# Attention and expert layers on one core: Q and K laid out transposed on the host, loaded where the scores read them, and the eighth applied to K in place

## The chip, the cores and the metric

The kernel runs on one core of a Trainium2 chip. The metric is device microseconds (us) of one execution. The time before the change is the median of three runs, 510.81 us (510.80 to 510.99). Engines are named as in the profile: PE is TensorE (PEld is its weight load), DVE is VectorE, ACT is ScalarE, POOL is GpSimd, SP is SyncE, which here only issues transfers.

## The reference

Three layers follow each other. Only the first is touched by the change.

```python
# attention: batch 2, 12 heads, 448 positions, 64 numbers per head
scores = (1 / sqrt(64)) * matmul(q, k.transpose(0, 1, 3, 2))   # the factor is 0.125, "the eighth"
scores = where(causal_mask, -1e9, scores)
attn = exp(scores - max(scores)) / (sum + 1e-9)
x = matmul(attn, v)                                            # then to 896 tokens x 768
# a top-1 layer of 8 experts: x -> gate * (relu(x @ w1[e]) @ w2[e])
# a dense layer: max(x @ w1, x @ w2, x @ w3) @ w_out
```

## The kernel before

The kernel has three stages on PE: attention (0 to about 131 us, with the first expert's first layer mixed into its end), the experts (to about 310 us) and the dense layer (to the end).

**Pairs.** Attention goes through 12 pairs of heads. K, Q and V come from the host as one tile per pair. `load(p)` (L455) makes the tiles `kr` and `qr` (112 partitions, 4 blocks of positions, 2 heads of 64) and issues their transfers from SP (L462); `loadv(p)` (L464) issues that of `vr`. A transfer into a tile that is used again waits on SP until its last reader is done, and everything behind it on SP waits too: transfers of the next pairs, of V, of the dense layer's first weights (token `D..x`) and of the experts' weights (`L0`, `L1`).

**Transposes.** The scores need both operands with the 64 head numbers on the partitions. `tk` (L473) transposes K in four blocks on PE into a PSUM bank, `tk_out` (L479) copies it to the tile `kt` (128 partitions: two heads of 64, 448 positions) by ACT or DVE (`put`, L483 to L487). `tq` (L489) does the same with Q, and `tq_out` (L495) copies it in two halves, times 0.125, into `qbd`: a block-diagonal tile of 7 blocks of 128 x 128, head 0 in the upper left quarter of each block, head 1 in the lower right one, so that one matmul serves both heads. There are three `qbd` tiles, used in turn; their other quarters are zeroed once (L434, L439), the whole tile being cleared.

**Scores and softmax.** `scores` (L510) multiplies the blocks of `qbd` with the front part of `kt`, in four groups (token `S0` to `S3`), and adds the mask. `row_max` on DVE (`M`), `row_exp` on ACT (`E`) and `row_rec` on DVE (`R`) follow, then `nrm` (`N0` to `N6`, L540), which divides a block of rows in place: on DVE, or on POOL where the token ends in p. `ptr` (`T0` to `T3`, L544) transposes the result on PE in four groups, `ptr_out` (`t`) copies it out, `av` (`A`) multiplies with V, `xtok` (`X`) transposes back, and `xtok_out` (L581) copies and sends the tokens to DRAM through POOL's queue (L587).

**Order.** Nothing is planned by the program: `SCHEDULE` (L18) is an order written by hand, one line for each step of the loop at L770, and every engine works its own instructions off in that order. A token is a digit (which pair, counted from the line's base `max(p - 2, -1)`), a letter (the function, chosen in `emit` at L724) and an argument (the group, then the PSUM tag or the engine). `1Qa 1K 1qss 1ks` is thus: transpose Q and K of pair 0, copy Q by ACT twice, copy K by ACT. `EA` and `EM` prepare the router's expert vectors on DVE and ACT. Before the loop, pairs 0 to 3 are loaded (L693 to L702); line p loads pair p + 3 and V of pair p + 2.

```python
    for p, line in enumerate(SCHEDULE[:-1]):
        if 0 < p < NP - 3:
            load(p + 3)
        if 2 <= p < NP - 2:
            loadv(p + 2)
        for tok in line.split():
            emit(max(p - 2, -1), tok)
```

Of the kernel before, what the change touches and what calls it, by code (L numbers as in the profile page):

```python
# [7 lines left out]
F32 = mybir.dt.float32  # L8
# [7 lines left out]


SCHEDULE = (  # L18
# [19 lines left out]
def kernel(  # L38
# [15 lines left out]
    nc = tc.nc  # L54
# [31 lines left out]
    def bank(tag, name, bufs=None):  # L86
        return ps.tile([P, 512], F32, tag=tag, name=name, bufs=bufs)
# [341 lines left out]
        poff.append(o)  # L429
        o += P * ((i + 2) // 2)  # L430
    PW = o
    qbd = [eb.tile([P, NQ, P], F32, name=f"qbd{i}") for i in range(3)]
    prb = [p.tile([P, PW], F32, name=f"prb{i}") for i, p in enumerate((eb, ab))]
    nc.vector.memset(qbd[0], 0.0)  # L434
    for t in prb:
        for i in range(0, NQ, 2):
            nc.vector.memset(t[:, poff[i] + 64 * (i + 1):poff[i] + 64 * (i + 2)], 0.0)
    for t in qbd[1:]:
        nc.gpsimd.memset(t, 0.0)  # L439

    pairs = [(b, hp) for b in range(B) for hp in range(HP)]
    NP = len(pairs)
# [11 lines left out]

    def load(p):  # L455
        b, hp = pairs[p]
        kr = eb.tile([TB, 4, 2, D], F32, tag="kr", name="kr", bufs=3)
        qr = eb.tile([TB, 4, 2, D], F32, tag="qr", name="qr", bufs=3)
        vr = ab.tile([P, 4, 2, D], F32, tag="vr", name="vr", bufs=4)
        raw[p] = (kr, qr, vr)  # L460
        for t, s in ((kr, k), (qr, q)):
            nc.sync.dma_start(out=t.rearrange("p c j d -> p (c j d)"), in_=s[p])  # L462

    def loadv(p):  # L464
        b, hp = pairs[p]
        vr = raw[p][2]
        nc.sync.dma_start(out=vr.rearrange("p c j d -> p (c j d)"), in_=v[p])

    held = {}

    BUFS = {"t": 3, "h": 1, "a": 2, "b": 2}

    def tk(p, tag):  # L473
        kr = raw[p][0]
        ps = held["k", p] = bank(tag, "psk", BUFS[tag])
        for c in range(4):
            nc.tensor.transpose(ps[:, c * TB:(c + 1) * TB], kr[:, c].rearrange("p j d -> p (j d)"), ident[:TB, :TB])

    def tk_out(p, eng):  # L479
        ktt[p] = eb.tile([P, S], F32, tag="kt", name="kt", bufs=3)  # L480
        put(eng, ktt[p], held.pop(("k", p))[:, :S])

    def put(eng, out, in_):  # L483
        if eng == "v":
# [1 line left out]
        else:  # L486
            nc.scalar.copy(out=out, in_=in_)  # L487

    def tq(p, tag):  # L489
        qr = raw[p][1]  # L490
        ps = held["q", p] = bank(tag, "psq", BUFS[tag])
        for c in range(4):
            nc.tensor.transpose(ps[:, c * TB:(c + 1) * TB], qr[:, c].rearrange("p j d -> p (j d)"), ident[:TB, :TB])

    def tq_out(p, eng):  # L495
        ps = held.pop(("q", p))
        t = qbd[p % 3]
        for h in range(2):
            r = slice(64 * h, 64 * h + 64)
            x = ps[r, :S].rearrange("p (i c) -> p i c", c=64)  # L500
            if eng[h] == "v":
                nc.vector.tensor_scalar(out=t[r, :, r], in0=x, scalar1=0.125, scalar2=None, op0=ALU.mult)
            else:
                nc.scalar.mul(out=t[r, :, r], in_=x, mul=0.125)

    SG = ((6,), (5, 0), (4, 1), (3, 2))
    SC = {6: 0, 5: 1, 0: 2, 4: 3, 1: 4, 3: 5, 2: 6}
# [2 lines left out]
    def scores(p, g, tag):  # L510
        if p not in sms:
            sms[p] = sm_p.tile([P, 3, 8], F32, tag="sm", name="sm")
        ps = held["s", p, g] = bank(tag, "pss", BUFS[tag])
        for i in SG[g]:
            n, o = 64 * (i + 1), SO[i]
            nc.tensor.matmul(ps[:, o:o + n], lhsT=qbd[p % 3][:, i], rhs=ktt[p][:, :n], start=i == SG[g][0], stop=False, skip_group_check=True)  # L516
        for i in SG[g]:
            o = SO[i] + 64 * i
            nc.tensor.matmul(ps[:, o:o + 64], lhsT=identb, rhs=maskb, start=False, stop=i == SG[g][-1], skip_group_check=True)  # L519
# [35 lines left out]
    done = {}  # L555

    def av(p, kt, tag):
        vr = raw[p][2]
        if kt == 0:
            held["a", p] = bank(tag, "psa", BUFS[tag])  # L560
            done[p] = 0
        ps = held["a", p]
        nb = NQ - 2 * kt
        base = sum(NQ - 2 * n for n in range(kt))
        kk = 64 if kt == 3 else P
        done[p] += 1
        for j in range(2):
            nc.tensor.matmul(ps[64 * j:64 * j + 64, P * kt:S], lhsT=vr[:kk, kt, j],
                             rhs=ptt[p][:kk, base:base + nb, 64 * j:64 * j + 64],
                             start=(kt == 0), stop=(done[p] == 4), skip_group_check=True)  # L570
# [153 lines left out]
    def emit(p, tok):  # L724
# [5 lines left out]
        elif tok[0] == "W":  # L730
            wsplit(int(tok[1]), int(tok[2]), int(tok[3]), tok[4])
        elif tok[0] == "D":
            u, c = int(tok[1]), 384 * int(tok[2])
            if tok[3:] == "":
                held[tok] = dw_dec(u, held.pop(tok + "a"), c, c + 384, 384)
            elif tok[3] == "a":
                held[tok] = magnitude(dwt[u][0], c, c + 384, 384)
            elif tok[3] == "l":
                held.pop(tok[:3])()
            else:  # L740
                dw_load(u)
        elif tok[0] == "H":
            held["S0"].L1(int(tok[1]), [int(tok[2])])
        else:
            p += int(tok[0])
            f, a = tok[1], tok[2:]
            if f == "S":
                scores(p, int(a[0]), a[1:] or "t")
            elif f == "M":
                row_max(p, int(a))  # L750
            elif f == "E":
                row_exp(p, int(a))
            elif f == "R":
                row_rec(p)
            elif f == "N":
                nrm(p, int(a[0]), nc.gpsimd if a[1:] else nc.vector)
            elif f == "T":
                ptr(p, int(a[0]), a[1:] or "a")
            elif f == "t":
                ptr_out(p, int(a[0]), a[1])  # L760
            elif f in "KQX":
                {"K": tk, "Q": tq, "X": xtok}[f](p, a or "b")
            elif f == "A":
                av(p, int(a[0]), a[1:] or "b")
            elif f == "q":
                tq_out(p, a)
            else:
                {"k": tk_out, "a": av_out, "x": xtok_out}[f](p, a)

    for p, line in enumerate(SCHEDULE[:-1]):  # L770
        if 0 < p < NP - 3:
# [327 lines left out]
def packed(name, a):  # L1099
# [1 line left out]
    import numpy as np  # L1101

    if name in ("q", "k"):
        a = a.reshape(2, 6, 2, 4, 112, 64).transpose(0, 1, 4, 3, 2, 5).reshape(12, 112, 512)
    elif name == "v":
        a = np.pad(a.reshape(2, 6, 2, 448, 64), ((0, 0), (0, 0), (0, 0), (0, 64), (0, 0)))
        a = a.reshape(2, 6, 2, 4, 128, 64).transpose(0, 1, 4, 3, 2, 5).reshape(12, 128, 512)
# [31 lines left out]
```

## Time and profile before

| | us |
|---|---|
| median of three runs | 510.81 |
| the profiled execution, own time | 510.31 |
| its span, first to last instruction | 508.6 |
| PE busy in the span | 487.9 (96%) |
| DVE busy | 334.2 (66%) |
| ACT busy | 280.0 (55%) |
| POOL busy | 47.5 (9%) |

The profiled execution is 0.50 us below the median, and 1.7 us of it lie outside the span. A row of a group of instructions gives their count, busy time and the mean duration of one; a row of the waits gives who waited for whom; a row of the timeline gives the start, the busy time and the number of instructions merged into it; a row of windows gives each engine's busy time in a stretch, with the number of instructions in brackets, the granted PE clock, the share of the DMA engines and GB/s.

### The profile page before, as it was taken

What the parts mean: (1) busy time and instruction counts of PE and PEld (TensorE: products, weight loads), DVE (VectorE), ACT (ScalarE), POOL (GpSimd) and SP (SyncE); (2) the same over time, 40 slices, a digit from 0 to 9 for tenths busy, and PEclk for the clock granted to TensorE, in tenths of its full rate; (3) what the DMA queues carried; (4) which work ended last, traced back from release to release, by engine and by line L of the source; (5) the groups of instructions that cost most, each with busy time, mean ns of one, the idle gap of its engine ahead of it and who ended that gap; (6) DMA issues with size and microseconds to landing.
All of it is one profiled execution on the core that took longest, in us unless ns stands there. A gap on an engine that the chain in (4) does not pass through costs nothing. (4 is left out here: it accounts for less than half of the span.)

```text
span 508.6 us, 8597 instructions
## 1 busy us (share of the span) xinstructions
PE 487.9 (96%) x2858; PEld 423.4 (83%) x2858; DVE 334.2 (66%) x692; ACT 280.0 (55%) x587; POOL 47.5 (9%) x71
## 2 busy tenths in 40 slices
PE   5999999999999999999999999699999999999994
PEld 4777676776789899889889888599999999999994
DVE  4899857997556398511398891489899898841000
ACT  5878878988643598623588882444453444411000
POOL 4321111211100000000011000000000000000111
PEclk9999999999999999999999999799999999999998
DMA  8552343931013798113898850744353440000111
GB/s 208 156 196 75 97 131 113 399 130 39 18 64 101 308 336 301 43 32 112 307 327 329 327 218 3 301 152 172 124 188 132 149 153 1 1 0 32 63 63 62
DMA packets 17788, 75.83 MB, mean 149 GB/s; under 512 B 2360, under 2 KB 2360, under 8 KB 17728
## 3 DMA queue, kind: packets, MB, share of 16 engines
q1 hardware_dynamic: 15328, 65.31, 36.3%
q0 software_dynamic: 2400, 9.83, 5.8%
q8 instruction: 24, 0.39, 0.3%
q14 instruction: 36, 0.29, 0.2%
HBM read 69.62 MB, written 5.51 MB: 148 GB/s over the span
## 5 line engine op out<-in xcount | busy, mean ns | idle before, releaser
L965 PE MATMUL pm<-x2h,dwh 128*128 128x448 f32 x204 | 75.0, 367 | 0.0
L967 PE MATMUL pm<-x2h,dwl 128*128 128x448 f32 x204 | 74.5, 365 | 0.0
L966 PE MATMUL pm<-x2l,dwh 128*128 128x448 f32 x204 | 74.4, 365 | 0.0
L971 PE MATMUL l<-w2h,hh 128*128 128x384 f32 x160 | 56.4, 352 | 0.7 <-ACT hh L207 0.7
L971 PE MATMUL l<-w2l,hh 128*128 128x384 f32 x160 | 53.8, 336 | 0.0
L242 DVE TENSOR_TENSOR w1l<-raw,w1h 128x768 fp32r<-128x768 f32 x40 | 36.4, 952 | 24.1 <-PE l L971 19.7
L516 PE MATMUL pss<-kt,qbd 128*128 128x320 f32 (+6 forms) x168 | 46.7, 397 | 1.3 <-ACT prb L530 1.3
L971 PE MATMUL l<-w1h,xhp 128*128 128x512 f32 x109 | 43.9, 403 | 0.0
L530 ACT ACTIVATE prb<-pss,sm 128x64 f32<-128x64 f32 (+6 forms) x84 | 39.5, 480 | 6.8 <-DVE sm L523 6.5
L971 PE MATMUL l<-w1l,xhp 128*128 128x512 f32 x109 | 43.2, 396 | 0.0
L967 PEld LDWEIGHTS pm<-x2h,dwl 128*128 128x128 f32 x204 | 38.2, 187 | 3.7
L174 ACT CAST dwh<-dt_t 128x768 fp32r<-128x768 f32 (+1 forms) x20 | 15.5, 773 | 46.6 <-DVE dt_t L173 46.6
L966 PEld LDWEIGHTS pm<-x2l,dwh 128*128 128x128 f32 x204 | 38.3, 188 | 3.3
L965 PEld LDWEIGHTS pm<-x2h,dwh 128*128 128x128 f32 x204 | 38.3, 188 | 3.2
L523 DVE TENSOR_REDUCE sm<-pss 128x1 f32<-128x448 f32 (+6 forms) x84 | 31.6, 414 | 9.7 <-PE pss L519 9.2
L971 PE MATMUL l<-w2h,hl 128*128 128x384 f32 x160 | 36.4, 337 | 0.3 <-DVE hl L210 0.3
L242 DVE TENSOR_TENSOR w2l<-raw,w2h 128x768 fp32r<-128x768 f32 x40 | 35.2, 952 | 0.9 <-ACT w2h L241 0.7
L516 PEld LDWEIGHTS pss<-kt,qbd 128*128 128x128 f32 x168 | 28.6, 194 | 8.5 <-ACT prb L530 1.8
L241 ACT CAST w1h<-raw 128x768 fp32r<-128x768 f32 x40 | 32.1, 844 | 0.0
L971 PE MATMUL l<-w1h,xlp 128*128 128x512 f32 x109 | 31.3, 394 | 0.0
L971 PEld LDWEIGHTS l<-w2h,hh 128*128 128x128 f32 x160 | 30.1, 188 | 1.4 <-ACT hh L207 1.0
L971 PEld LDWEIGHTS l<-w2l,hh 128*128 128x128 f32 x160 | 30.2, 189 | 0.4
(263 smaller groups left out, 1009.8 us busy)
## 6 DMA issues: line engine op xcount, KB each, us to landing
raw<-in_moe_w_dram SPq DMA_DIRECT2D x48, 768.0 KB, 7.2
rawd<-in_moe_w_dram SPq DMA_DIRECT2D x18, 768.0 KB, 5.4
rawd<-in_moe_w_out_dram SPq DMA_DIRECT2D x6, 768.0 KB, 5.3
vr<-in_v_dram SPq DMA_DIRECT2D x12, 256.0 KB, 4.9
kr<-in_k_dram SPq DMA_DIRECT2D x12, 224.0 KB, 4.4
qr<-in_q_dram SPq DMA_DIRECT2D x12, 224.0 KB, 3.4
xd<-xall POOLq DMA_DIRECT2D x12, 224.0 KB, 3.1
xrp<-xd,idx POOLq DMA_INDIRECT x11, 5.1
```

Source lines behind the costliest of these rows:

```text
L174: nc.scalar.copy(out=hi[:, c0:c1], in_=f)
L241: nc.scalar.copy(out=hi[:, sl], in_=r[:, sl])
L242: nc.vector.tensor_tensor(out=lo[:, sl], in0=r[:, sl], in1=hi[:, sl], op=ALU.subtract)
L516: nc.tensor.matmul(ps[:, o:o + n], lhsT=qbd[p % 3][:, i], rhs=ktt[p][:, :n], start=i == SG[g][0], stop=False, skip_group_check=True)
L523: nc.vector.tensor_reduce(out=sms[p][:, 0, SC[i]:SC[i] + 1], in_=held["s", p, g][:, SO[i]:SO[i] + 64 * (i + 1)], axis=AX.X, op=ALU.max, ne ...
L530: nc.scalar.activation(out=prb[p % 2][:, poff[i]:poff[i] + n], in_=ps[:, SO[i]:SO[i] + n], func=AF.Exp, bias=sm[:, 0, SC[i]:SC[i] + 1], sc ...
L965: nc.tensor.matmul(o, lhsT=lh, rhs=rh, start=first, stop=False)
L966: nc.tensor.matmul(o, lhsT=lh, rhs=rl, start=False, stop=False)
L967: nc.tensor.matmul(o, lhsT=ll, rhs=rh, start=False, stop=last)
L971: nc.tensor.matmul(o, lhsT=a, rhs=b, start=first and n == 0, stop=last and n == len(ops) - 1)
```

## The change

K and Q come from the host with the 64 head numbers on the rows (12 x 128 x 448). K's transfer writes `kt` itself, now in four buffers; two transfers write the two quarters of `qbd`, of which there are four, in pieces of 64 numbers. The transposes and their copies go. The factor 0.125 is applied to `kt` in place by a new function `scale` (token `q`): on DVE for pairs 0 and 1, on POOL for the ten others, where it stands first in its line (`4qp`, for the pair loaded one line earlier; `3qp` in line 0). Only the quarters of `qbd` that stay zero are cleared: two half-tile memsets for each of the four, on DVE for the first, on POOL for the others.

```diff
-    "1Qa 1K 1qss 1ks EA 2K 1S0 1M0 2Qa EM 2ks 1S1 1E0 2qss 1M1 1E1 1S2 1M2 1E2 3Kh 1S3 3kv 1M3 1E3 2S0a 3Qh",
-    "2M0 1R 1N2p 1N1 2S1 2M1 2E0 3qss 4K 2E1 2S2 1N0 1N6p 1N3 2M2 4ks 1N4 1N5 4Qh 1T0 2S3 1T1b 1t0v D00x 2M3 4qss 2E2 3S0 ET 1T3 1t1s",
+    "1qv 2qv 3qp EA 1S0 1M0 EM 1S1 1E0 1M1 1E1 1S2 1M2 1E2 1S3 1M3 1E3 2S0a",
+    "4qp 2M0 1R 1N2p 1N1 2S1 2M1 2E0 2E1 2S2 1N0 1N6p 1N3 2M2 1N4 1N5 1T0 2S3 1T1b 1t0v D00x 2M3 2E2 3S0 ET 1T3 1t1s",
...
-    qbd = [eb.tile([P, NQ, P], F32, name=f"qbd{i}") for i in range(3)]
+    qbd = [eb.tile([P, NQ, P], F32, name=f"qbd{i}") for i in range(4)]
...
-    nc.vector.memset(qbd[0], 0.0)
+    for n, t in enumerate(qbd):
+        for j in range(2):
+            (nc.gpsimd if n else nc.vector).memset(t[64 * j:64 * j + 64, :, 64 - 64 * j:128 - 64 * j], 0.0)
...
-    for t in qbd[1:]:
-        nc.gpsimd.memset(t, 0.0)
...
-        kr = eb.tile([TB, 4, 2, D], F32, tag="kr", name="kr", bufs=3)
-        qr = eb.tile([TB, 4, 2, D], F32, tag="qr", name="qr", bufs=3)
-        vr = ab.tile([P, 4, 2, D], F32, tag="vr", name="vr", bufs=4)
-        raw[p] = (kr, qr, vr)
-        for t, s in ((kr, k), (qr, q)):
-            nc.sync.dma_start(out=t.rearrange("p c j d -> p (c j d)"), in_=s[p])
+        ktt[p] = eb.tile([P, S], F32, tag="kt", name="kt", bufs=4)
+        raw[p] = ab.tile([P, 4, 2, D], F32, tag="vr", name="vr", bufs=4)
+        nc.sync.dma_start(out=ktt[p], in_=k[p])
+        for j in range(2):
+            r = slice(64 * j, 64 * j + 64)
+            nc.sync.dma_start(out=qbd[p % 4][r, :, r], in_=q[p, r].rearrange("d (i c) -> d i c", c=64))
...
-    def tk(p, tag):
-    def tk_out(p, eng):
-    def tq(p, tag):
-    def tq_out(p, eng):
...
+    def scale(p, eng):
+        e = nc.vector if eng == "v" else nc.gpsimd
+        e.tensor_scalar(out=ktt[p], in0=ktt[p], scalar1=0.125, scalar2=None, op0=ALU.mult)
...
-            nc.tensor.matmul(ps[:, o:o + n], lhsT=qbd[p % 3][:, i], rhs=ktt[p][:, :n], start=i == SG[g][0], stop=False, skip_group_check=True)
+            nc.tensor.matmul(ps[:, o:o + n], lhsT=qbd[p % 4][:, i], rhs=ktt[p][:, :n], start=i == SG[g][0], stop=False, skip_group_check=True)
...
     if name in ("q", "k"):
-        a = a.reshape(2, 6, 2, 4, 112, 64).transpose(0, 1, 4, 3, 2, 5).reshape(12, 112, 512)
+        a = a.reshape(2, 6, 2, 448, 64).transpose(0, 1, 2, 4, 3).reshape(12, 128, 448)
```

In the other lines of `SCHEDULE` the tokens `K`, `Q`, `k` and the old `q` are taken out and `4qp` is put first (lines 1 to 9); the order of the rest stays.

## Rows read from the trace of the kernel before

**Rows 1.** Windows of the attention stage: engines in order PE, PEld, DVE, ACT, POOL.
```profile
0.00:16.00 16.00, 10.77 (x58) 8.00 (x59) 8.52 (x29) 10.08 (x27) 5.92 (x25) 1.00 0.87 219
16.00:33.00 17.00, 16.99 (x127) 12.28 (x125) 14.28 (x40) 13.62 (x42) 5.40 (x6) 1.00 0.54 169
33.00:52.00 19.00, 19.00 (x144) 13.84 (x144) 17.75 (x51) 15.36 (x47) 4.38 (x5) 1.00 0.30 89
52.00:69.00 17.00, 17.00 (x128) 12.23 (x127) 14.58 (x42) 13.71 (x41) 2.98 (x4) 1.00 0.44 126
69.00:90.40 21.40, 20.08 (x159) 14.09 (x155) 14.16 (x60) 17.71 (x52) 3.26 (x4) 1.00 0.39 130
```
**Rows 2.** Waits of PE from 0 to 180 us: total, times, longest.
```profile
PE pss L516 <- ACT prb L530: 1.3, 2, 0.8
PE pst L550 <- ACT pt L487: 1.2, 1, 1.2
```
**Rows 3.** PE's timeline at a group of transposes and what follows it.
```profile
48.63 0.58 PE L477 MATMUL psk<-ident,kr 112*128 112x112 f32 x4
49.05 1.06 PE L516 MATMUL pss<-kt,qbd 128*128 128x384 f32 x4
```
**Rows 4.** Windows of the tiles alone (PE, PEld, DVE, ACT): psk twice, psq.
```profile
0.00:18.70 18.70, 3.12 (x16) 2.24 (x16) 0.61 (x1) 1.60 (x3) 1.00 0.89 233
...
33.00:52.00 19.00, 1.16 (x8) 0.79 (x8) 0.62 (x1) 0.66 (x2) 1.00 0.30 89
...
0.00:18.70 18.70, 3.15 (x16) 2.16 (x16) 0.00 (x0) 3.59 (x7) 1.00 0.89 233
```
**Rows 5.** The copies of the tiles psk and psq: ns min/median/max, first and last start.
```profile
L487 ACT COPY kt<-psk x9: 527/533/572, 6.5 to 90.5; 128x448 f32<-128x448 f32 x9
L485 DVE COPY kt<-psk x3: 615/615/618, 13.0 to 41.6; 128x448 f32<-128x448 f32 x3
...
L504 ACT ACTIVATE qbd<-psq x23: 526/539/552, 5.3 to 98.7; 64x448 f32<-64x448 f32 x23
```
**Rows 6.** Normalisation L540 by shape (0 to 111 us), and on DVE from 15.8 to 18.8 us.
```profile
L540 POOL TENSOR_SCALAR prb<-prb,sm 128x448 f32<-128x448 f32 x2 | 3.1, 1550 | 0.0
...
L540 DVE TENSOR_SCALAR prb<-prb,sm 128x320 f32<-128x320 f32 x8 | 3.0, 378 | 0.0
...
L540 DVE TENSOR_SCALAR prb<-prb,sm x5: 245/347/706, 15.9 to 18.0; 128x128 f32<-128x128 f32 x1, 128x64 f32<-128x64 f32 x1, 128x256 f32<-128x256 f32 x1, 128x320 f32<-128x320 f32 x1
```
**Rows 7.** K's transfers: time on SP; then those of 2.52 and 6.14 us, last number us to landing.
```profile
L462 SPq DMA_DIRECT2D kr<-in_k_dram x12: 312/426/445, 0.8 to 71.4; - x12
...
kr<-in_k_dram SPq DMA_DIRECT2D x1, 224.0 KB, 4.4
...
kr<-in_k_dram SPq DMA_DIRECT2D x1, 224.0 KB, 7.5
```
**Rows 8.** DMA queues by packets, MB, share of 16 engines: 44 to 48, 114 to 120, 3 to 5 us.
```profile
q1 hardware_dynamic: 400, 0.72, 60.4%
...
q0 software_dynamic: 80, 0.23, 14.9%
...
q1 hardware_dynamic: 309, 0.32, 75.1%
```
**Rows 9.** The start: timeline of DVE (two) and ACT (two).
```profile
4.40 0.95 DVE L141 TENSOR_TENSOR hp<-er 8x768 f32<-8x768 f32 x1 [1.88 <-DMA er<-in_moe_expert_emb_dram]
...
15.47 0.17 DVE L535 TENSOR_SCALAR sm<-sm 128x7 f32<-128x7 f32 x1 [0.30 <-ACT prb L530]
...
8.55 1.28 ACT L530 ACT_TABLE_LOAD   x1
...
10.86 1.08 ACT L504 ACTIVATE qbd<-psq 64x448 f32<-64x448 f32 x2
```
**Rows 10.** Timeline of POOL's first normalisation and of PE's second group of transposes T.
```profile
16.08 2.45 POOL L540 TENSOR_SCALAR prb<-prb,sm 128x192 f32<-128x192 f32 x2 [9.02 <-DVE sm L536]
...
18.77 0.63 PE L550 MATMUL pst<-ident,prb 128*128 128x128 f32 x4
```

More of the change, by code (lines that the diff above doesn't have):

```diff
@@ L456, in load @@
         b, hp = pairs[p]
-        kr = eb.tile([TB, 4, 2, D], F32, tag="kr", name="kr", bufs=3)
-        qr = eb.tile([TB, 4, 2, D], F32, tag="qr", name="qr", bufs=3)
-        vr = ab.tile([P, 4, 2, D], F32, tag="vr", name="vr", bufs=4)
-        raw[p] = (kr, qr, vr)
-        for t, s in ((kr, k), (qr, q)):
-            nc.sync.dma_start(out=t.rearrange("p c j d -> p (c j d)"), in_=s[p])
+        ktt[p] = eb.tile([P, S], F32, tag="kt", name="kt", bufs=4)
[4 more added lines that the diff above has]
+            nc.sync.dma_start(out=qbd[p % 4][r, :, r], in_=q[p, r].rearrange("d (i c) -> d i c", c=64))
     def loadv(p):
         b, hp = pairs[p]
-        vr = raw[p][2]
+        vr = raw[p]
         nc.sync.dma_start(out=vr.rearrange("p c j d -> p (c j d)"), in_=v[p])
@@ L471 @@
     BUFS = {"t": 3, "h": 1, "a": 2, "b": 2}
-    def tk(p, tag):
[L474 to L477, printed above, removed]
-    def tk_out(p, eng):
-        ktt[p] = eb.tile([P, S], F32, tag="kt", name="kt", bufs=3)
-        put(eng, ktt[p], held.pop(("k", p))[:, :S])
     def put(eng, out, in_):
@@ L487, in put @@
             nc.scalar.copy(out=out, in_=in_)
-    def tq(p, tag):
[L490 to L493, printed above, removed]
-    def tq_out(p, eng):
[L496 to L504, printed above, removed]
+    def scale(p, eng):
+        e = nc.vector if eng == "v" else nc.gpsimd
+        e.tensor_scalar(out=ktt[p], in0=ktt[p], scalar1=0.125, scalar2=None, op0=ALU.mult)
     SG = ((6,), (5, 0), (4, 1), (3, 2))
@@ L557, in av @@
     def av(p, kt, tag):
-        vr = raw[p][2]
+        vr = raw[p]
         if kt == 0:
@@ L760, in emit @@
                 ptr_out(p, int(a[0]), a[1])
-            elif f in "KQX":
-                {"K": tk, "Q": tq, "X": xtok}[f](p, a or "b")
+            elif f == "X":
+                xtok(p, a or "b")
             elif f == "A":
@@ L765, in emit @@
             elif f == "q":
-                tq_out(p, a)
+                scale(p, a)
             else:
-                {"k": tk_out, "a": av_out, "x": xtok_out}[f](p, a)
+                {"a": av_out, "x": xtok_out}[f](p, a)
     for p, line in enumerate(SCHEDULE[:-1]):
```

18 rows, old and new, of the table SCHEDULE are left out of this document.

## The prediction, made before the changed kernel was run

> **What bounds the kernel now.** I read the windows of the attention stage first, then PE's waits, then PE's timeline, and last the start and the DMA queues. In the windows the reader is to see that PE is busy for the whole of 16 to 69 us, while ACT and DVE are not [rows 1]; DVE is close behind in 33 to 52 us, at 17.75 of 19 us. The waits say the same: up to 180 us PE loses 1.3 us to banks that ACT has not emptied yet, and 1.2 us to a copy by ACT [rows 2]. PE's busy time could hide waiting, so I looked at starts: a group of four transposes begins at 48.63 us and the next scores at 49.05 [rows 3]. A group thus takes 0.42 us of PE, and nothing stands idle around it. Only the first 16 us are otherwise: PE has 10.77 us of work there and DMA is 87% busy [rows 1].
>
> **What goes from PE.** Twelve pairs with four transposes of K and four of Q are 96, or 24 groups. 16 of each kind lie before 18.7 us [rows 4], so 64, or 16 groups, after it: 16 x 0.41 = **6.6 us** (0.41 as the mean of several such pairs of starts). The eight earlier groups I count at nothing: until then the transfers and the order of DVE and ACT set the pace (below); if that cover were gone they would be worth up to 3.3 us.
>
> **What goes from ACT and DVE.** ACT loses 9 copies of K at 0.53 us and 23 half copies of Q at 0.54 us, 17.2 us in all; DVE loses three copies of K at 0.615 us and one half of Q [rows 5]. In 69 to 90.4 us ACT works 17.71 of 21.4 us [rows 1], and there its lateness costs PE the 1.3 us [rows 2]. With about 1.6 us per pair less work it should no longer be late, but DVE may be instead: I take **1.0 us** of the 1.3, between 0 and 1.3. The 1.2 us come at the end of attention, where no transposes of Q and K lie, and stay.
>
> **What DVE pays.** In 33 to 52 us PE loses two groups of K [rows 4] and as many of Q, 1.7 us, and would need 17.3 us; DVE's 17.75 fall by one copy to 17.1. So DVE becomes nearly the bound in that stretch; it can't be fed without gaps, and I take 1.0 us back there, and nothing in the other stretches, where it has more than 2 us to spare now. POOL's new work is ten scalings of 128x448 at 1.55 us [rows 6], and DVE works in the same memory. The row nearest to a collision: while POOL normalised at 16.08 to 18.53 us, one of DVE's normalisations took 706 ns, where the largest shape in that window, 128x320, has a mean of 378 [rows 6]. That is 0.33 us for one DVE instruction. At 0.33 us per scaling, ten cost DVE 3.3 us, of which only those count that fall where DVE is the bound; most scalings stand ahead of R, where DVE has few such instructions. I take 0.5 us. The sum for DVE is **1.5 us back**, with bounds of 0 and 5 (all of the 1.7 and of the 3.3). [...]
>
> **The transfers.** A pair now needs three SP issues, not two, some 0.43 us each [rows 7]; in the steady lines SP has time. K and Q write tiles that the scores of four pairs earlier read. So `load(p + 3)` at the head of line p waits on SP for the last scores of pair p - 1, late in line p - 1; V, the dense layer's first weights and later the experts' weights stand behind it. V already waits for the middle of line p, and what stands behind V with it; K is then nearly a line ahead of its scaling, some 8 us, against 4.4 to 7.5 us to landing [rows 7] in a crowded queue. I cost that at nothing; it costs only if landing took a line. Q is written in 896 pieces of 256 B. No row shows such pieces. The lower bound is the price by bytes: V, K and Q at 60.4% of 16 engines for 4 us are 38.7 engine-us for 0.72 MB, or 0.8 us for one 224 KB tile [rows 8]. The nearest row by size is the tokens' transfer, 448 pieces of 512 B in 14.9% of 16 x 6 us, 32 ns a piece; 896 of them would be 1.8 us, 1.0 more than now. The upper bound is the stretch with a broadcast of 4-byte pieces, 309 packets in 75.1% of 16 x 2 us, 78 ns a packet [rows 8]: 4.4 us, 3.6 more. As the tokens' row fits the price by bytes as well, I take half of 1.0, **0.5 us per pair**. [...]
>
> **The start.** There DMA is the bottleneck. DVE now scales K of pair 1 before the expert vectors (`2qv 3qp EA 1S0 1M0`), and DVE and ACT keep that order. K of pair 1, issued at 2.52 us, landed 4.4 us later, at 6.9 [rows 7]; with one issue more ahead of it and 0.5 us for Q it lands at 7.9. Scaling ends at 8.4, the two vector steps (0.95 us each, which ran from 4.40 on before [rows 9]) at 10.3; ACT's square root and the table load of 1.28 us follow, so that the table is there near 11.8, not at 9.83. The two copies of Q between the exps (1.08 us at 10.86 us [rows 9]) are gone, so the reciprocal of pair 0 moves only from 15.47 to about 15.6. The cleared quarters cost what the cleared tiles did, within 1 us, beside the transfers. Next, POOL: `4qp` stands ahead of `1N2p`. K of pair 3 landed at 6.14 + 7.5 = 13.6 us [rows 7]; with three Qs ahead of it, 15.1, so its scaling ends at 16.7 and the normalisation starts then, not at 16.08. PE's second group of T waits for the end of that normalisation even now (18.53, then 18.77 [rows 10]), so it starts **0.7 us later**, with bounds of -0.7 (the two copies go, the pieces cost their bytes) and +9.9 (K lands at 13.6 + 3 x 3.6 = 24.4, scaled at 26.0).
>
> **The sum.** -6.6 - 1.0 + 1.5 + 0.7 = -5.4 us on the profiled execution's 510.31, so 504.9. It lies 0.5 us under the median of 510.81; I predict **505.4**. Behind attention no wait of PE is longer than those named up to 180 us, and what starts earlier ends earlier.
>
> **The rivals.**
> - *The start starves.* Pieces at 32 to 50 ns, K of pair 3 at 17 to 20 us, the second group 2 to 5 us late: about 507.7. For it: DMA at 87% in the first 16 us. Against it: the tokens' row costs no more per byte.
> - *The pieces cost as much as the smallest packets* (slower). The same queue at 78 ns a piece: POOL's normalisation waits until 26.0 us, 9.9 us late, against 6.1 us won later: 510.31 - 6.1 + 9.9 + 0.5 = 514.6. It turns slower where the extra per pair exceeds about 2.3 us, some 55 ns a piece. Against it: 4 B are far from 256.
> - *The scaling shuts DVE out* for its whole 1.55 us. The 36 us from 33 to 69 hold about four lines, 9.0 us of PE and 8.1 of DVE each [rows 1]; DVE would need 9.5, 0.5 more than a line now, nine times: about 515. It decides above 1.1 us per scaling; the row shows 0.33.
> - *DVE is already the bound*, and the lines keep their length: 510.5. For it: 33 to 52 us. Against it: 14.28 of 17 and 14.16 of 21.4 us [rows 1].
> - *All of it arrives.* No loss on DVE, the start 0.7 early: -6.6 - 1.3 - 0.7, so 502.2.
>
> **How the numbers follow.** Chances: forecast 0.60 (503.5 to 507), starved start 0.13, all arrives 0.12, costly pieces 0.06, DVE shut out 0.04, DVE the bound 0.05. The range takes in forecast, starved start and all arrives, 502.0 to 509.5. A measurement can tell 0.2%, 1.0 us, from no change. Faster by more: these three, less 0.01, is 0.84; the same: 0.06; slower: 0.10.
>
> **What the profile would show.** Right: no L477 and L493, PE busy without a gap from about 21 us on, no wait of PE for ACT near 86 us, the second group of T near 19.5 us, attention ending 5 us earlier, nothing else moved. Wrong: PE waiting for DVE in 33 to 52 us by more than 1.5 us; POOL's first scaling of line 1 ending after 18 us; DVE's normalisations at 1.5 us and over; or PE waiting for K, Q or the first expert's weights.

## The result, and the profile after

The changed kernel takes **503.3 us** (median of four runs, 502.25 to 504.91) against 510.9 of the kernel before in the same runs: ratio 0.9853, interval 0.983 to 0.9877. Run again beside the kernel before, it took 502.41 (502.36 to 504.18; before 510.6), ratio 0.9851, 0.9833 to 0.9869. The profiled execution is the slowest of the first four, 504.91 with a span of 502.6; the spans of the four, 502.6, 502.3, 500.8 and 500.5, go with mean granted clocks of 0.987, 0.990, 0.993 and 0.993.

The stretches of attention after the change, against [rows 1] (PE, PEld, DVE, ACT, POOL, clock, DMA share, GB/s):

```profile
0.00:16.00 16.00, 9.06 (x31) 5.57 (x31) 8.63 (x30) 6.68 (x19) 9.59 (x31) 0.89 0.77 205
16.00:33.00 17.00, 16.00 (x117) 11.02 (x116) 14.80 (x41) 10.24 (x35) 8.36 (x8) 1.00 0.62 181
33.00:52.00 19.00, 18.67 (x134) 13.05 (x133) 18.63 (x53) 13.77 (x44) 6.82 (x7) 1.00 0.39 99
52.00:69.00 17.00, 17.00 (x122) 11.09 (x123) 15.65 (x43) 11.40 (x39) 6.26 (x7) 1.00 0.43 117
69.00:90.40 21.40, 20.16 (x155) 14.07 (x152) 16.82 (x65) 17.56 (x54) 7.40 (x7) 1.00 0.54 182
```

PE is still what bounds it. But where it was busy for 35.99 of 36 us from 16 to 52, it now has gaps of 1.0 and 0.33 us, and DVE is busy for 18.63 of 19 us. What ends the gaps, against [rows 2] (PE's waits in the whole execution: total, times, longest):

```profile
PE pss L493 <- DMA qbd<-in_q_dram: 4.8, 1, 4.8
PE pm L948 <- ACT x2h L203: 3.4, 1, 3.4
PE pss L493 <- ACT prb L507: 2.6, 2, 2.1
...
PE psa L545 <- DVE pt L475: 0.7, 1, 0.7
PE psa L545 <- ACT pt L477: 0.6, 1, 0.6
PE pst L527 <- DVE pt L475: 0.3, 1, 0.3
...
PE pst L527 <- DVE prb L517: 0.2, 1, 0.2
```

Of the 1.3 us that PE lost to late exps by ACT [rows 2], 0.5 are left (2.6 less the 2.1 of the start). The 0.7 and 0.3 us for DVE's copies and the 0.6 us for one by ACT are new.

Where the time went is best read at places that both kernels have: the start of a certain PE instruction in the timelines.

| us | before | after | again | difference, after |
|---|---|---|---|---|
| second group of T | 18.77 | 18.45 | 19.57 | -0.3 |
| token transposes (psm) of the first pair | 27.95 | 27.20 | 28.13 | -0.8 |
| those of the last pair | 128.65 | 124.35 | 125.28 | -4.3 |
| experts' last matmul issued, then PE waits | 317.32 | 313.12 | 313.94 | -4.2 |
| that wait, for ACT's x2h | 5.21 | 3.37 | 3.16 | -1.8 |
| span | 508.6 | 502.6 | 502.4 | -6.0 |

The rows of the last pair and of the end of that wait, before and then after:

```profile
128.65 0.60 PE L579 MATMUL psm<-ident,xt 128*112 128x128 f32 x4
...
322.53 0.74 PE L971 MATMUL pm<-x2h,dwh 128*128 128x448 f32 x1 [5.21 <-ACT x2h L203]
...
124.35 0.60 PE L556 MATMUL psm<-ident,xt 128*112 128x128 f32 x4
...
316.49 0.74 PE L948 MATMUL pm<-x2h,dwh 128*128 128x448 f32 x1 [3.37 <-ACT x2h L203]
```

So the gain has **two parts**. 4.2 us come from attention and travel through the experts unchanged. 1.8 us come from one wait, at the start of the dense layer, where the change touches nothing. The profiled execution's own time fell by 5.4 us and not by 6.0, since 2.3 us of it lie outside the span, against 1.7 before. The medians fell by 7.6 and 8.2 us, more than the profiles account for.

Of the start, two rows of DVE, two of ACT, two of POOL and one of PE (timeline of after):

```profile
6.84 0.39 DVE L481 TENSOR_SCALAR kt<-kt 128x448 f32<-128x448 f32 x1 [2.94 <-DMA kt<-in_k_dram]
...
15.61 0.16 DVE L512 TENSOR_SCALAR sm<-sm 128x7 f32<-128x7 f32 x1
...
9.48 1.28 ACT L507 ACT_TABLE_LOAD   x1
10.77 0.63 ACT L507 ACTIVATE prb<-pss,sm 128x448 f32<-128x448 f32 x1
...
13.33 1.33 POOL L481 TENSOR_SCALAR kt<-kt 128x448 f32<-128x448 f32 x1 [2.21 <-DMA kt<-in_k_dram]
16.18 2.47 POOL L517 TENSOR_SCALAR prb<-prb,sm 128x192 f32<-128x192 f32 x2 [1.52 <-DVE sm L513]
...
18.91 0.55 PE L527 MATMUL pst<-ident,prb 128*128 128x128 f32 x3 [0.16 <-DVE prb L517]
```

K of pair 1 is there by 6.84, K of pair 3 by 13.33 us. POOL's normalisation waits for DVE's reciprocal and not for POOL's own scaling, and starts at 16.18 (16.08 in [rows 10]).

### The profile page after: what moved, and what is told of

Same layout as the page of the kernel before. It is cut to its first block, busy times and chain, and to the rows that moved or that the text cites. A ratio compares the mean times of both kernels' runs of the same rounds, so it can differ in the third digit from the quotient of the medians.

```text
span 502.6 us, 8406 instructions
## 1 busy us (share of the span) xinstructions
PE 480.7 (96%) x2762; PEld 414.8 (83%) x2762; DVE 335.7 (67%) x691; ACT 264.2 (53%) x555; POOL 62.6 (12%) x85
## 3 DMA queue, kind: packets, MB, share of 16 engines
q1 hardware_dynamic: 25120, 65.31, 37.4%
## 5 line engine op out<-in xcount | busy, mean ns | idle before, releaser
L493 PE MATMUL pss<-kt,qbd 128*128 128x320 f32 (+6 forms) x168 | 49.1, 417 | 7.6 <-DMA qbd<-in_q_dram 4.8
L1070 POOL DMA_INDIRECT out_dram<-ob,sidx x7 | 6.9, 980 | 198.0 <-DVE ob L1069 198.0
L527 PE MATMUL pst<-ident,prb 128*128 128x128 f32 x192 | 29.7, 281 | 1.8 <-ACT pt L477 1.2
```

Source lines behind the costliest of these rows:

```text
L493: nc.tensor.matmul(ps[:, o:o + n], lhsT=qbd[p % 4][:, i], rhs=ktt[p][:, :n], start=i == SG[g][0], stop=False, skip_group_check=True)
L527: nc.tensor.transpose(ps[:, n * P:(n + 1) * P], prb[p % 2][:, poff[i] + kt * P:poff[i] + (kt + 1) * P], ident)
L1070: nc.gpsimd.indirect_dma_start(out=out, out_offset=bass.IndirectOffsetOnAxis(ap=sidx[:, t:t + 1], axis=0), in_=ob, in_offset=None)
```

## The experiments

Every kernel was compared with the kernel before on its own chip. In the table, "T" is the start of the second group of T, "X1 to X12" the time from the first pair's token transposes to the last's, "waits" what PE waited in between, "x2h" its wait behind the experts.

| kernel | median us | ratio (interval) | T | X1 to X12 | waits | x2h |
|---|---|---|---|---|---|---|
| before (first profile) | 510.81 | | 18.77 | 100.70 | 2.53 | 5.2 |
| before_again | 510.91 | 1.0007 (0.9998 to 1.0016) | 19.33 | 100.68 | 2.52 | 5.4 |
| before_pad | 509.28 | 0.9973 (0.9964 to 0.9982) | 19.48 | 100.66 | 2.54 | 3.1 |
| k_only | 507.22 | 0.9934 (0.9919 to 0.9949) | 17.80 | 101.44 | 5.31 | 3.5 |
| k_only_sq | 504.90 | 0.989 (0.9874 to 0.9906) | 18.28 | 99.16 | 3.14 | 3.3 |
| q_only | 504.08 | 0.9874 (0.9859 to 0.989) | 17.71 | 98.41 | 2.66 | 3.3 |
| after | 503.30 | 0.9853 (0.983 to 0.9877) | 18.45 | 97.15 | 3.41 | 3.4 |
| again | 502.41 | 0.9851 (0.9833 to 0.9869) | 19.57 | 97.15 | 3.36 | 3.2 |
| act_pad | 504.75 | 0.9885 (0.9865 to 0.9905) | 18.09 | 97.95 | 3.55 | 3.6 |
| ea_first | 503.29 | 0.9864 (0.9847 to 0.9882) | 17.55 | 97.06 | 3.35 | 3.3 |
| scale_act | 502.67 | 0.9846 (0.9821 to 0.9871) | 17.13 | 96.78 | 2.80 | 3.2 |
| best | 500.48 | 0.9806 (0.979 to 0.9823) | 15.57 | 96.74 | 2.75 | 3.3 |
| best_sq | 499.77 | 0.9791 (0.9777 to 0.9805) | 14.96 | 96.36 | 2.35 | 3.2 |
| noscale | 499.57 | 0.9795 (0.9779 to 0.981) | 15.03 | 96.28 | 2.77 | 3.1 |

**again: the changed kernel once more**, no edit.

> The changed kernel once more, for a second profile. [...]

X1 to X12 agrees to 0.01 us; what differs between two profiles of one kernel lies in the start, where T moved by 1.1 us, and behind the experts. Differences of some tenths in X1 to X12 thus mean something, and differences of 1 us in T do not. The end of attention moved by 0.94 us (127.58 to 128.52). The recorded clock does not show why: in the first profile it reads 0.50 from 12 to 14 us and 0.70 from 14 to 16, here 1.00, and the scores are slow all the same (a row of windows with all engines as above, then PE's timeline):

```profile
14.00:16.00 2.00, 2.00 (x5) 0.88 (x4) 0.98 (x3) 1.04 (x5) 1.17 (x1) 1.00 1.06 255
...
15.04 1.95 PE L493 MATMUL pss<-kt,qbd 128*128 128x384 f32 x4
```

Before the change the same four scores took 0.99 us, at 14.77. Nor is a spread the changed kernel's alone: its first four runs spread over 2.7 us (502.25 to 504.91), and beside these here the kernel before spread over 2.1 us (509.19 to 511.3).

**ea_first: the expert vectors and the first scores ahead of the second scaling on DVE.**

```diff
-    "1qv 2qv 3qp EA 1S0 1M0 EM 1S1 ...",
+    "1qv EA 1S0 1M0 2qv 3qp EM 1S1 ...",
```

> The expert vectors (EA) and the first row maximum are put ahead of the scaling of pair 1's K on DVE. Theory (order): the start is set by DVE and ACT's order, as EA stands behind a transfer that it doesn't need; the first exp begins near 9.0 us, not 10.77, the reciprocal of pair 0 near 14.3, not 15.6, and the kernel is 0.8 to 1.5 us faster than the changed kernel. Rival (transfers): the start is set by the transfers of K of pair 3 and POOL's queue; the second group of softmax transposes begins at 18.5 us as before and the time stays within 0.3 us.

The start follows DVE's order: the first exp begins at 8.61 us, not 10.77, and the reciprocal of pair 0 at 12.74, not 15.80. Attention ends at 126.33 instead of 127.58 and 128.52 us. The gain of 0.8 to 1.5 us does not show in the time, which is not told apart from after's. The early start runs into the next wait, POOL's:

```profile
PE pst L527 <- POOL prb L517: 2.0, 1, 2.0
...
PE pst L527 <- DVE prb L517: 0.9, 1, 0.9
```

Now POOL's scaling of pair 3, which stands ahead of its normalisation, is what PE waits for: the place that the prediction named, reached only once the wait in front of it is gone.

**noscale: the scaling left out.**

```diff
     def scale(p, eng):
-        e = nc.vector if eng == "v" else nc.gpsimd
-        e.tensor_scalar(out=ktt[p], in0=ktt[p], scalar1=0.125, scalar2=None, op0=ALU.mult)
+        return
```

> The factor 0.125 is left out altogether, so scores are eight times too large; every other instruction stays. Theory (port): the ten scalings on POOL hold DVE's instructions; without them DVE's integer steps L171 to L173 return from 472, 673 and 637 ns to 361, 563 and 558, PE's waits for DVE at 31 and 38 us go, and the kernel is 0.8 to 2.0 us faster. Rival (DVE's own work): POOL's scaling costs nothing, DVE's remaining work sets the pace; within 0.4 us, all of that from the two scalings on DVE at the start.

T comes at 15.03 instead of 18.45 and 19.57 us, and X1 to X12 is 0.87 us shorter. The twelve scalings thus cost 2.8 to 3.7 us (against the medians of again and after), where 0.8 to 2.0 were expected; 0.9 of it is paid between X1 and X12, where seven of POOL's ten scalings lie. PE's wait of 0.7 us for DVE near 31 us goes, that of 0.3 near 38 us stays. DVE's steps L171 to L173 return to 360, 564 and 558 ns, as the theory said. That DVE is held there shows also in its normalisations from 15.9 to 107 us (shape, count, busy time and mean ns): before,

```profile
L540 DVE TENSOR_SCALAR prb<-prb,sm 128x384 f32<-128x384 f32 x10 | 4.6, 461 | 0.0
...
L540 DVE TENSOR_SCALAR prb<-prb,sm 128x128 f32<-128x128 f32 x9 | 2.7, 303 | 0.1
```

after,

```profile
L517 DVE TENSOR_SCALAR prb<-prb,sm 128x384 f32<-128x384 f32 x11 | 5.5, 502 | 0.0
...
L517 DVE TENSOR_SCALAR prb<-prb,sm 128x128 f32<-128x128 f32 x10 | 3.7, 365 | 0.1
```

and without the scaling:

```profile
L516 DVE TENSOR_SCALAR prb<-prb,sm 128x384 f32<-128x384 f32 x11 | 4.8, 437 | 0.0
...
L516 DVE TENSOR_SCALAR prb<-prb,sm 128x128 f32<-128x128 f32 x9 | 2.7, 300 | 0.0
```

The two means rise by 41 and 62 ns with POOL's scalings and fall back without them. These are the two shapes of seven that rise most; 128x64 rises by 40 ns, the other four by 17 or less. By what means the scalings lengthen them no run shows: "port", the name of this theory and the next, was the author's guess. In the rival of the forecast a scaling shuts DVE out for all of its time, here 1.43 us (median of POOL's ten in after). Ten of those would be 14 us of DVE; the trace shows nothing of that size.

**scale_act: pairs 3 to 11 scaled by ACT.**

```diff
-    "4qp 2M0 1R 1N2p ...",
+    "4qs 2M0 1R 1N2p ...",
...
+        if eng == "s":
+            nc.scalar.mul(out=ktt[p], in_=ktt[p], mul=0.125)
+            return
```

> Pairs 3 to 11 are scaled on ACT, at the same place of each line, instead of POOL. Theory (port): ACT has the time (it works some 13 us of 17 to 19), so most of what leaving the factor out gives comes here too: 0.5 to 1.5 us faster than the changed kernel, DVE's steps at their old durations. Rival (ACT's order): 0.53 us nine times ahead of the exps of each line put ACT back where it was before the change; no faster, with PE waiting for ACT near 83 us for over 1 us.

X1 to X12 falls by 0.37 us and T comes 1.3 us earlier than in after's profile. DVE's steps L171 to L173 take their old 361, 563 and 558 ns again, as in noscale. The rival's wait of PE for ACT near 83 us stays at 0.5. The time, 502.67, is not told apart from after's, so the expected 0.5 to 1.5 us are not shown.

**before_again: the kernel before once more.**

> The kernel before, unchanged, for the spread of its own readings. Theory (the 1.8 us behind the experts belong to the change): its wait of TensorE for ScalarE's x2h is again about 5.2 us, and the stretch from the second transpose group of the softmax to the end of attention again about 113.1 us. Rival (they are chance of one profile): the wait is 3 to 4 us here, as in the five profiles of changed kernels.

X1 to X12 again agrees to 0.02 us, and the wait for x2h is 5.4 us: it is no chance of one profile.

**act_pad: ScalarE's instructions brought back to their old number.**

```diff
+    pad = const.tile([P, 1], F32, name="pad")
...
+        for _ in range(3 if p < 8 else 2):
+            nc.scalar.copy(out=pad, in_=ident[:, 0:1])
```

> After, with 32 ScalarE instructions of one column each added where the scalings are issued, so that ScalarE again has as many instructions as before (587); they write a column that nobody reads. Theory (the wait behind the experts follows where ScalarE's instructions lie, and the change moved them): the wait for x2h is back at about 5.2 us instead of 3.1 to 3.4, and the time 1.8 us above after's, about 504.5. Rival (it follows something else): the wait stays at 3.1 to 3.4 and the time at 502.4 to 503.3; the 32 small instructions cost ScalarE some 6 us beside other work and TensorE under 0.3 us.

The wait stays at 3.6 us, so the number of ACT's instructions does not set it: that theory fell, in this form. The time is 504.75, near the theory's 504.5 by chance and 2.3 us over again's. In the landmarks X1 to X12 is 0.8 us longer than in again, PE's way through the experts too (186.2 us from the end of attention to the wait, 185.4 in again), and the wait is 0.4 us longer, while T comes 1.5 us earlier; what lies behind the wait was not followed up.

**before_pad: the kernel before, with 18 idle instructions.**

```diff
     def tk_out(p, eng):
+        for _ in range(2 if p % 2 else 1):
+            nc.scalar.copy(out=pad, in_=ident[:, 0:1])
```

> Before, with 18 ScalarE instructions of one column added ahead of the copies of K; they write a column that nobody reads. For TensorE's wait for x2h behind the experts, 5.2 and 5.4 us in two profiles of before and 3.2 to 3.6 in all of eight changed kernels. Theory (it follows how ScalarE's instructions lie, a shift of any size can move it): 3 to 4 us here, and from the experts' end on as the changed kernels. Rival (it follows something that the change took away, not the place of the instructions): 5.2 to 5.4. TensorE may lose up to 2 us more in attention, where ScalarE is late already.

Adding work makes it **faster by 0.27%** (ratio of the runs; 1.2 us by the medians); its interval, up to 0.9982, leaves out 1. The place, first in the kernel before (ACT, then DVE):

```profile
321.91 2.43 ACT L203 CAST x2h<-x2T 128x448 fp32r<-128x448 f32 x5 [6.11 <-DVE y L278]
...
320.33 0.62 DVE L278 TENSOR_SCALAR y<-l,glast 128x384 f32<-128x384 f32 x1 [3.94 <-DVEq L991]
```

then with the idle instructions (ACT, DVE):

```profile
321.28 1.97 ACT L203 CAST x2h<-x2T 128x448 fp32r<-128x448 f32 x4 [4.06 <-DVEq L995]
...
321.62 0.62 DVE L278 TENSOR_SCALAR y<-l,glast 128x384 f32<-128x384 f32 x1 [3.81 <-DVEq L995]
```

and after the change (ACT):

```profile
315.88 2.43 ACT L203 CAST x2h<-x2T 128x448 fp32r<-128x448 f32 x5 [4.27 <-DVEq L968]
```

Both engines stand idle for about 4 us where the program passes from the experts to the dense layer. In the kernel before, ACT takes up work 1.6 us after DVE; in the others it is there as early as DVE. The x2h that ACT makes needs nothing from DVE's y, as the other kernels show, where it starts first; the releaser named in the row is only the last event before it. The 1.8 us thus need none of the parts of the change: 18 added instructions give them too (2.1 us less wait than before, with 0.8 us more in the experts, as in act_pad). That the change gains them in the same way is likely and not shown. What makes ACT late was not found; the number of instructions alone is ruled out by act_pad, which has ACT's old 587 and not the old wait.

**k_only: K alone laid out by numpy.**

```diff
-    "1Qa 1K 1qss 1ks EA 2K 1S0 ...",
+    "1Qa 1qss EA 1S0 ...",
...
+        ktt[p] = eb.tile([P, S], F32, tag="kt", name="kt", bufs=4)
+        nc.sync.dma_start(out=ktt[p], in_=k[p])
```

> K alone laid out by numpy; Q as before, through TensorE, with the eighth in its copy: no scaling on GpSimd, no pieces of 256 bytes. 8 of the 16 late groups of transposes go. Theory of the forecast (a group is worth 0.41 us): from the second transpose group of the softmax to attention's end 113.1 - 3.3 = 109.8 us. Rival (0.33 us, since TensorE's busy time fell by 5.2 to 5.4 us and not 6.6 for 16 groups): 110.5 us. Time 506 to 508.

Neither: from T to the end of attention it took 113.45 us (131.25 - 17.80), 0.3 more than before. Up to the sixth pair's token transposes K alone had won 2.67 us; at the seventh it was 0.62. In between ACT does this:

```profile
77.64 0.84 ACT L590 ACTIVATE xall<-xall 112x768 f32<-112x768 f32 x1 [2.97 <-DMA xd<-xall]
...
78.59 1.07 ACT L487 COPY pt<-pst 128x512 f32<-128x512 f32 x2
```

and PE this:

```profile
79.72 1.02 PE L568 MATMUL psa<-pt,vr 128*64 128x320 f32 x8 [2.18 <-ACT pt L487]
```

ACT's squares for the router overwrite the tokens of batch 0 (`xall`), which a transfer to memory is still reading. ACT waits for the end of that transfer, with the copy of the softmax behind it, and PE waits for the copy. Before the change the wait was 0.68 us and cost PE nothing:

```profile
78.02 0.85 ACT L590 ACTIVATE xall<-xall 112x768 f32<-112x768 f32 x1 [0.68 <-DMA xd<-xall]
```

The earlier PE and ACT get there, the more of it shows.

**k_only_sq: the same, with the squares written elsewhere.**

```diff
-        nc.scalar.activation(out=sqj if part else xall[b][:, c, d0:d1], ...
+        nc.scalar.activation(out=sqj if part else hp0[:TB, :DM] if b == 0 else xall[b][:, c, d0:d1], ...
```

> K alone, with the squares of batch 0 written to a tile that is free then instead of over their own input. Theory (K alone won nothing behind 70 us because ScalarE's squares, which overwrite what a transfer to memory is still reading, stood 3.0 us in its queue, with the copy behind them on which TensorE waited 2.2 us): ScalarE's wait for that transfer and TensorE's 2.2 us are gone, the stretch from the first token transposes to the last falls from 101.4 to about 99, the time by some 2 us to about 505.2. Rival (the copy is late for another reason): both stay.

As the theory said, to 0.3 us: 99.16, and 504.90. ACT goes on without a wait:

```profile
75.18 0.84 ACT L590 ACTIVATE hp<-xall 112x768 f32<-112x768 f32 x1
...
76.14 1.07 ACT L487 COPY pt<-pst 128x512 f32<-128x512 f32 x2
```

**q_only: Q alone, K through PE as before.**

```diff
-    "1Qa 1K 1qss 1ks EA 2K 1S0 ...",
+    "1K 1ks EA 2K 1S0 ...",
...
-        put(eng, ktt[p], held.pop(("k", p))[:, :S])
+        x = held.pop(("k", p))[:, :S]
+            nc.scalar.mul(out=ktt[p], in_=x, mul=0.125)
```

> Q alone laid out by numpy and written in pieces of 256 bytes; K as before, through TensorE, with the eighth in its copy: no scaling on GpSimd. 8 of the 16 late groups of transposes go. If a group's place on TensorE is worth 0.33 us and the pieces cost nothing, the token transposes of the first pair and of the last lie 8 x 0.33 = 2.6 us less apart than before (100.7 us), so 98.1; if the pieces' transfers are late, scores wait for a transfer into qbd after 18 us. Time 506 to 508, with the wait behind the experts at 3.5 us or at 5.3.

98.41, and no wait for a transfer into `qbd` behind the start. Between the two landmarks lie 7 groups of Q and not 8, so 0.33 us would have given 98.4. The time, 504.08, is better than expected: it holds the 1.8 us of the wait for x2h besides. Q alone, which needs no scaling of its own, thus lies only 0.8 us behind the whole change.

**best and best_sq: both edits of the start and the scaling, then the squares elsewhere.** best joins the diffs of ea_first and scale_act; best_sq adds that of k_only_sq.

> After, with the embeddings' square sum and the first scores ahead of the second scaling on VectorE, and the scalings of pairs 3 to 11 on ScalarE, GpSimd left with that of pair 2. Theory (the order of the start and GpSimd's scaling ahead of a normalisation each hold the second transpose group of the softmax, and not the later lines): that group at about 15.5 us instead of 18.5 to 19.6, the end of attention about 124.5 instead of 127.6 to 128.5, time about 500. Rival (the two gains are the same wait, counted twice): as the scalings on ScalarE alone, group at 17, attention's end at 126, 502.5.

> The version with the early first scores and ScalarE's scalings, with the squares of batch 0 written to a tile that is free then. Theory: TensorE's wait of 0.7 us for a copy by ScalarE at about 75 us goes, and with it up to 0.7 us of the time: about 499.8. Rival: the 0.5 us that TensorE then waits for an exponential grows by as much, and the time stays at 500.5.

best is faster than before and than after: 500.48, ratio 0.9806, its interval (up to 0.9823) just under that of after, which begins at 0.983. T comes at 15.57 us, so the two waits at the start are one behind the other, as expected, and not the same wait counted twice. It comes near the kernel that has no scaling (X1 to X12 96.74 against 96.28, T 15.57 against 15.03). best_sq shortens X1 to X12 by another 0.38 us: the wait of 0.7 us for ACT's copy is gone, PE waits 0.3 us for a normalisation by DVE at that place instead, and the 0.5 us for an exp stay. Its time is not told apart from best's.

## Why the prediction was right, and where it was not

The forecast was -5.4 us on the profiled execution, 505.4 for the median. The profiled execution fell by exactly 5.4 (510.31 to 504.91), and the medians, 503.3 and 502.41, lie in the range. That it fits so well is luck: the profiled execution was the slowest of its four, and **errors cancel** in it. The groups won 1.6 us less than forecast and the waits for ACT and DVE cost 0.5 more; the start was 1.0 better, a wait behind the experts fell by 1.8, and 0.6 more lie outside the span.

- **What goes from PE: the step that failed.** The 16 late groups were priced at 0.41 us each, 6.6 in all, by the distance from a group's start to the next start [rows 3]. Their removal brought 5.0: T to X12 fell from 109.88 to 105.90 us, 3.98, while the waits there grew by 1.04. The kernels with fewer side effects say the same: without waits, X1 to X12 fell by 4.66 us for 14 groups in noscale, by 2.42 for 7 of Q in q_only, by 2.15 for 7 of K in k_only_sq, so 0.33, 0.35 and 0.31 us a group. One place shows where the rest goes. Before, around a group of Q (PE's timeline):

```profile
45.74 0.55 PE L493 MATMUL psq<-ident,qr 112*128 112x112 f32 x4
46.12 0.60 PE L550 MATMUL pst<-ident,prb 128*128 128x128 f32 x4
46.56 0.92 PE L516 MATMUL pss<-kt,qbd 128*128 128x448 f32 x2
47.31 0.19 PE L519 MATMUL pss<-maskb,identb 128*128 128x64 bf16 x1
...
47.81 0.93 PE L516 MATMUL pss<-kt,qbd 128*128 128x320 f32 x4
```

After:

```profile
45.03 0.60 PE L527 MATMUL pst<-ident,prb 128*128 128x128 f32 x4
45.52 1.02 PE L493 MATMUL pss<-kt,qbd 128*128 128x448 f32 x2
46.37 0.19 PE L496 MATMUL pss<-maskb,identb 128*128 128x64 bf16 x1
...
46.87 0.93 PE L493 MATMUL pss<-kt,qbd 128*128 128x320 f32 x4
...
47.69 1.06 PE L493 MATMUL pss<-kt,qbd 128*128 128x384 f32 x4
```

The group took 0.38 us, but without it the next transposes need 0.49 instead of 0.44, and the scores behind them 0.85 instead of 0.75: 0.15 of 0.38 is given back. The place that the prediction had chosen [rows 3] gives nothing back: before, the group started 0.82 us after the scores ahead of it (47.81 to 48.63), now the next scores do (46.87 to 47.69), so that all of its 0.42 us are won. Site by site, from before to noscale and without new waits, six of the 14 groups between X1 and X12 give 0.39 to 0.42 us, five 0.31 to 0.36 and three 0.16 to 0.24. The distance from start to start thus was right for less than half of the sites and was taken for all.
- **ACT and DVE.** Forecast: 1.0 won of PE's waits for ACT, 1.5 lost to DVE, together +0.5. Measured: +1.0. Of ACT's 1.3 us 0.8 went, but 0.6 came for the copy behind the squares, a wait that the prediction did not look for, as it cost PE nothing before. DVE's share is 1.2 (0.7, 0.3 and 0.2), near the 1.5, but most of it falls in 16 to 33 us and only 0.3 in 33 to 52, where it was expected.
- **POOL's hold** was priced at 0.5 us, and noscale shows 0.9 for seven of the ten scalings; most of it is PE's wait of 0.7 us for DVE's copy, which noscale and scale_act do not have. The rival in which DVE is shut out falls.
- **The transfers.** Twelve pairs in 256-byte pieces raise the queue's share only from 36.3% to 37.4% for the same 65.31 MB:

```profile
q1 hardware_dynamic: 25120, 65.31, 37.4%
```

That is 0.374 x 502.6 x 16 - 0.363 x 508.6 x 16 = 54 engine-us, or 0.28 us per pair on 16 engines, half of the 0.5 taken, and K lands at 13.3 and not 15.1 us. Both rivals of the transfers fall. The pieces cost more than their bytes, by 0.28 us or about a third of the 0.8 us of a tile by bytes. SP pays instead: each of Q's two issues takes 617 ns (median), where 0.43 us were assumed. That puts the issue of pair 3's K from 6.14 to 8.85 us, and still it lands no later than before.
- **The start**: +0.7 forecast, -0.3 and +0.8 measured against the first profile of before, -0.9 and +0.2 against before_again: no shift is shown. The mechanism is another. The prediction read T as waiting for POOL's normalisation even before; PE was at work until T began, at 18.77:

```profile
18.72 0.22 PE L519 MATMUL pss<-maskb,identb 128*128 128x64 bf16 x2
```

After the change DVE's order and the exp table (10.77 and not 11.8 us) leave PE idle from 9.4 to 11.55 us, and its scores then run at a granted clock of 0.50 (12 to 14 us) and 0.70 (14 to 16 us). POOL's queue, which the prediction had made the limit, is only second. The eight early groups were also put at nothing for a reason that the trace does not bear out: from 8 to 18 us PE was busy for 9.99 of 10 us before. The new wait and the slow scores took up what their removal won. best, which has not this wait and whose scores take 1.00 to 1.06 us a group from 9.84 us on (1.54 to 1.95 ahead of that), has T at 15.57, 3.2 and 3.8 us earlier than the two profiles of before; that this is the 3.3 us which the prediction had named for these groups is likely and not shown.
- **"Behind attention ... what starts earlier ends earlier"** did not hold. The kernel before has a longer wait there, the 5.2 us for x2h, which the prediction passed over, and it fell by 1.8 us. before_pad shows such a fall without the change; its cause stays open. Without it the span would fall by 4.2 us, and the time would be some 505 (503.3 and 1.8, an estimate).

So what can be traced to the change is 4.2 us in the profiles, where 5.4 were forecast; the rest came from a place that the forecast left out.

## What to carry to other kernels

Price a removed PE group by what its neighbours do without it, not only by its own distance to the next start: part of it had covered what its successor now shows (0.15 of 0.38 us at one site here). Before an engine gets earlier, look for waits on it that cost nothing today, above all for a transfer that reads what the engine overwrites (0.68 us of ACT's time and none of PE's before, 2.97 and 2.18 in k_only). And compare two kernels at landmarks: a total that fits can be made of a step that was too dear and of a stall that merely moved, and an added idle instruction is a cheap test of the latter.

## What the runs showed of the hardware that was not expected

- **An idle time moves with instructions elsewhere in the program.** From the experts to the dense layer ACT and DVE stand idle some 4 us; ACT's part varied between 4.1 and 6.3 us with changes elsewhere in the program, and 18 added instructions made the kernel 1.2 us faster.
- **The granted clock after two idle times of PE.** After PE's idle time at the start of after, and around that behind the experts, the granted clock reads 0.50 for a while, then 1.00 (windows of after, PE alone: length, busy time, clock, DMA share, GB/s):

```profile
12.00:14.00 2.00, 2.00 (x7) 0.50 1.05 239
14.00:16.00 2.00, 2.00 (x10) 0.70 0.79 196
16.00:18.00 2.00, 1.89 (x15) 1.00 0.93 235
316.50:322.50 6.00, 6.00 (x19) 0.51 0.93 353
324.00:330.00 6.00, 6.00 (x31) 1.00 0.79 327
```

How long it reads 0.50 differs between executions of the same program: behind the experts, by windows of 1 us from PE's start there (one that reads between 0.50 and 1.00 counted in part), 5.9 us in after and 3.4 in again, 5.7 and 6.2 us in the two profiles of before, and 3.4 in before_pad. At 0.50, the 2.5 us more of after against again cost some 1.2 (an estimate, half of 2.5). That this and the start make up the 2 us by which runs of one kernel differ is not shown. At the start the record is not whole: again's scores are slow at a recorded 1.00, and in act_pad PE stands idle for 1.78 us at the same place and then takes 1.00 us for the two scores of 128x448, at 12.56, where after takes 1.84.
